# Second half of the tokens: second layer by seven block products over pairs of chunks, with stored first-layer weights

## The chip, the cores and the metric

The kernel runs on one NeuronCore of a Trainium2 chip. The metric is device time in microseconds (us) of one execution, the median of several runs. In the profile PE is TensorE (matmuls), PEld its weight loads, DVE VectorE, ACT ScalarE, POOL GpSimd and SP SyncE, which issues the DMAs here.

## What is computed

Clustered attention, then two feed-forward stages. The attention output (2 batches x 768 tokens, 8 heads x 64, so 1536 x 512) goes through a dense layer pair (512 to 2048, squared relu, 2048 to 512). The change touches the last stage alone, a mixture of 4 experts in which every token goes to every expert:

```python
def _moe2_ref(x, domain_probs, w1, w2):      # x 1536 x 512, w1 4 x 512 x 1024, w2 4 x 1024 x 512
    p = domain_probs / (domain_probs.sum(-1, keepdims=True) + 1e-09)
    out = np.zeros((N, D), dtype=np.float32)
    for e in range(E):
        h = np.maximum(x @ w1[e], 0.0)
        out += p[:, e:e + 1] * (h @ w2[e])
    return out
```

All is float32. A factor is split into a high half in the matmul's own format (fp32r) and a low half, the rest, and a product is made of three matmuls: high x high, high x low, low x high.

## The kernel before

In the last stage the tokens are done in two halves of 768, one after the other (NFQ = 16 chunks each, n = 0 to 15 and 16 to 31). A chunk is 256 of an expert's 1024 hidden columns; four chunks make an expert. For each chunk there is a group (`group`, L1652):

- **First layer**: the 512 x 256 weight block and the 768 tokens are cut into 2 x 2 blocks and multiplied by seven block products in place of eight (`PROD`, L890; `product`, L1023; `block_product`, L895). One is six matmuls of 384 columns. Chains A, B and C accumulate several products in one PSUM bank each, and ACT (`c_copy`, L1033) and DVE (`c_add`, L1036) take intermediate results out of them. Relu and the split into halves follow (`h_hi`, L1042, on ACT; `h_lo`, L1045, on DVE), into the tiles ga and gb.
- **Second layer**: six token tiles of 128 tokens (`token_tile`, L1080; `tile_products`, L1056), each six matmuls of 512 columns, and then an eviction on DVE (L1093) that multiplies by the token's probability and adds to the accumulator tile x2. The last one of all is split (`last_tile`, L1065).
- **Weights**: `fq_load` (L974) has SP load the chunk's two blocks into the tile raw. `fq_prep` (L992) makes the first layer's operands: plain blocks on ACT (L1005) and POOL (L1006), four sums on POOL (`w_sums`, L195), mixed blocks on ACT (L207) and POOL (L208). They lie in W["X"] and W["Y"], each with two halves by the parity of n. `second_hi` (L1014) and `second_lo` (L1017) split the second layer's block into W["Z"].

The second half of the tokens runs the same sixteen chunks again, weights included. Its first-layer token operands (`r_hi`, L967; `r_lo`, L970; tiles xa and rt) are made near the end of the first half; `swapped` (L1629) makes the last two in group 16, as products 4 and 3 of chunk 15 free their places.

The order of all instructions is written out by hand: each engine runs its own in the order in which the program issues them. In a group it is: products 4, (1), 3 of the chunks n - 1, n, n - 1; then 5, 6, 2, 7 of n; then the six token tiles of n - 1, with the preparation of chunk n + 1 between them. So products 3 and 4 of chunk n come one group later than its others:

```python
product(n, 1)                       # L1657
...
token_tile(n - 1, 0)                # L1681, behind product 7 of n
...
fq_load(n + 3, 0)                   # L1692
fq_load(n + 2, 1)
```

Of the kernel before, what the change touches and what calls it, by code (L numbers as in the profile page):

```python
# [34 lines left out]
def moe_attention_kernel(  # L35
# [178 lines left out]
    with tc.manual_schedule():  # L214
# [849 lines left out]

        def last_tile():  # L1065
            n, t = 2 * NFQ - 1, NTT - 1
            j = 2 * NTT - 1
            pc = pe_p[:, j, NFQ // NQ - 1:NFQ // NQ]
            acc, d = acc_j(1, t), ov[1, t].rearrange("p (a n) -> p a n", a=2)
            for m, (a, c0, c1) in enumerate(((0, 0, 256), (1, 0, 128), (1, 128, 256))):  # L1070
                o = bank[(7, 0, 2)[m]][:, 0:c1 - c0]
                tile_products(n, t, o, slice(a * 256 + c0, a * 256 + c1))
                x = acc[:, a, c0:c1]
                nc.vector.scalar_tensor_tensor(
                    out=x, in0=o, scalar=pc, in1=x, op0=ALU.mult, op1=ALU.add)
                if m != 1:
                    nc.sync.dma_start(
                        out=d[:, a] if m else d[:, 0], in_=acc[:, a])
# [618 lines left out]
        NN = 2 * NFQ  # L1697
        for n in range(NN):
# [44 lines left out]
```

## Time and profile before

| | us |
|---|---|
| median of 3 runs | 1007.53 |
| lowest and highest | 1006.74, 1007.82 |
| the profiled execution | 1007.97 |
| its span, first to last instruction | 1006.0 |
| granted TensorE clock | 0.999 of 2.4 GHz |

The span has roughly these stages: attention until about 250 us, the dense layer pair until about 505, the first half of the tokens in the last stage until about 744, and the second until the end. All times of the rows below count from the span's start. An entry of a list of groups has busy time, mean duration in ns, and the idle time ahead of it with what ended it; a duration holds the instruction's start and end phases, which overlap with its neighbours'.

### The profile page before, as it was taken

Reading aid. Unit: us, or ns where it says so; the run is one execution under the profiler, and the core shown is the slowest. Engines: PE = TensorE matmul, PEld = TensorE weight load, DVE = VectorE, ACT = ScalarE, POOL = GpSimd, SP = SyncE. Lnnn points to the kernel's source line nnn. Section 1 sums busy time; section 2 is a strip of 40 time slices with the busy share of each in tenths; the row PEclk is TensorE's granted clock in tenths of the full one; section 3 lists DMA queues with packets and bytes.
Section 4 is the critical chain, followed back from the end, with each engine's and each line's share of the span. In section 5 each row is a group of like instructions: output and inputs, shape, how many; then the busy total and the mean of one; then the engine's idle time right before and its main releaser. Section 6 shows DMA issues by size and latency. Waiting matters only on the chain.

```text
span 1006.0 us, 15008 instructions
## 1 busy us (share of the span) xinstructions
PE 998.3 (99%) x5469; PEld 893.7 (89%) x5469; DVE 734.4 (73%) x1126; ACT 560.2 (56%) x1131; POOL 607.8 (60%) x618
## 2 busy tenths in 40 slices
PE   8999999999999999999999999999999999999998
PEld 8999999999888888888889989899899898998997
DVE  6898999888899997898585555567676555555555
ACT  6888888888655654446554344344453443444431
POOL 6468777763326604347576766767678567676671
PEclk9999999999999999999999999999999999999999
DMA  7577876862112122212012212122123221221201
GB/s 186 128 157 178 205 172 165 178 140 72 42 43 84 45 82 84 85 42 83 22 43 85 61 65 84 42 85 65 62 84 119 71 84 43 84 67 60 84 22 63
DMA packets 74082, 89.65 MB, mean 89 GB/s; under 512 B 27332, under 2 KB 50264, under 8 KB 74008
## 3 DMA queue, kind: packets, MB, share of 16 engines
q1 hardware_dynamic: 74008, 88.69, 31.9%
q8 instruction: 43, 0.70, 0.3%
q14 instruction: 31, 0.25, 0.1%
HBM read 62.58 MB, written 3.19 MB: 65 GB/s over the span
## 4 chain that ended last, share of the span: by engine, by line
PE 95%; DVE 2%; POOL 1%; DMA 1%; ACT 1%; issue 0%; SPq 0%; POOLq 0%; ACTq 0%
PE bank L900 29%; PE bank L1062 26%; PE bank L931 13%; PE s L656 6%; PE t L689 6%; PE bank L878 5%; PE po L703 3%; PE po L705 3%; PE s L878 1%; PE m L478 1%; PE m L393 1%; PE po L1114 0%; DMA k<-nkh 0%; PE m L494 0%; DVE ptl L695 0%
## 5 line engine op out<-in xcount | busy, mean ns | idle before, releaser
L1093 DVE SCALAR_TENSOR_TENSOR x<-bank,pe_p,x 128x512 f32<-128x512 f32 x179 | 134.3, 751 | 67.4 <-PE bank L1062 67.2
L1006 POOL TENSOR_TENSOR wxl<-raw,wxh 128x512 fp32r<-128x512 f32 x64 | 82.5, 1310 | 139.7 <-ACT wxh L1005 139.7
L207 ACT CAST wyh<-raw 128x512 fp32r<-128x512 f32 x64 | 39.6, 621 | 152.0 <-POOL raw L200 120.4
L1062 PE MATMUL bank<-wzh,ga 128*128 128x512 f32 (+1 forms) x392 | 121.9, 386 | 0.0
L1062 PE MATMUL bank<-wzh,gb 128*128 128x512 f32 x384 | 121.2, 390 | 0.0
L1037 DVE TENSOR_TENSOR fa<-bank,fa 128x384 f32<-128x384 f32 x96 | 53.3, 556 | 85.5 <-PE bank L900 56.4
L695 DVE TENSOR_TENSOR ptl<-t,pth 128x384 fp32r<-128x384 f32 x192 | 98.1, 549 | 20.0 <-ACT pth L694 19.6
L900 PE MATMUL bank<-xa,wxh 128*128 128x384 f32 (+1 forms) x392 | 103.9, 346 | 0.0
L665 DVE TENSOR_REDUCE nb<-s 128x1 f32<-128x768 f32 x96 | 90.9, 948 | 8.4 <-PE s L656 8.0
L694 ACT CAST pth<-t 128x384 fp32r<-128x384 f32 x192 | 83.9, 486 | 9.3 <-PE t L689 8.4
L900 PE MATMUL bank<-xa,wyh 128*128 128x384 f32 (+1 forms) x344 | 88.6, 338 | 0.0
L676 ACT ACTIVATE p<-s,nb 128x768 f32<-128x768 f32 x96 | 88.0, 916 | 0.3 <-DVE nb L665 0.2
L656 PE MATMUL s<-k,q 80*128 80x384 f32 (+1 forms) x384 | 86.5, 346 | 0.2
L1062 PEld LDWEIGHTS bank<-wzh,ga 128*128 128x128 f32 x392 | 73.3, 188 | 14.5
L689 PE MATMUL t<-identf,p 128*128 128x128 f32 x576 | 85.4, 276 | 0.4 <-DVE ptl L695 0.3
L1062 PEld LDWEIGHTS bank<-wzh,gb 128*128 128x128 f32 x384 | 72.1, 188 | 14.7
L208 POOL TENSOR_TENSOR wyl<-raw,wyh 128x512 fp32r<-128x512 f32 x64 | 84.6, 1342 | 0.0
L1034 ACT COPY fa<-bank 128x384 f32<-128x384 f32 x96 | 46.1, 480 | 66.1 <-PE bank L900 66.0
L703 PE MATMUL po<-pth,vv 128*128 128x256 f32 x288 | 80.4, 309 | 0.0
L931 PE MATMUL bank<-gb,wzh 128*128 128x512 f32 x240 | 78.0, 391 | 0.2
L900 PEld LDWEIGHTS bank<-xa,wxh 128*128 128x128 f32 x392 | 72.2, 188 | 5.6
L689 PEld LDWEIGHTS t<-identf,p 128*128 128x128 f32 x576 | 67.6, 140 | 9.5 <-DVE ptl L695 6.8
(290 smaller groups left out, 2640.8 us busy)
## 6 DMA issues: line engine op xcount, KB each, us to landing
raw<-in_moe_w_dram SPq DMA_DIRECT2D x64, 512.0 KB, 3.6
raw<-in_moe_w_in_dram SPq DMA_DIRECT2D x7, 1024.0 KB, 5.2
raw<-in_moe_w_out_dram SPq DMA_DIRECT2D x6, 1024.0 KB
k<-nkh SPq DMA_DIRECT2D x28, 192.0 KB, 3.3
q<-nqh SPq DMA_DIRECT2D x28, 192.0 KB, 4.1
nv<-in_v_dram SPq DMA_DIRECT2D x16, 192.0 KB, 4.1
out_dram<-x SPq DMA_DIRECT2D x11, 256.0 KB, 2.0
k<-nkl SPq DMA_DIRECT2D x14, 192.0 KB, 3.4
```

Source lines behind the costliest of these rows:

```text
L208: return lambda: eng.tensor_tensor(lo, a[m], hi.bitcast(F32), op=ALU.subtract)
L656: nc.tensor.matmul(s[:, j, 0:HALF], stk[i, nq][:, t * 128:(t + 1) * 128], stk[i, nk][:, j * HALF:(j + 1) * HALF], start=first, stop=not first)
L665: nc.vector.tensor_reduce(out=nb, in_=s_ps[u][:, :, 0:HALF], axis=AX.XY, op=ALU.max, negate=True)
L676: nc.scalar.activation(p, s_ps.pop(u)[:, :, 0:HALF], AF.Exp, bias=nb_t.pop(u), accum_out=sums_t[hp][:, i % 2, t:t + 1])
L689: nc.tensor.transpose(tp[:, j], p_sb[u][:, half, j * 128:(j + 1) * 128], identf)
L694: return (lambda: nc.scalar.copy(dh, tp), lambda: nc.vector.tensor_tensor(dl, tp, dh.bitcast(F32), op=ALU.subtract))
L695: lambda: nc.vector.tensor_tensor(dl, tp, dh.bitcast(F32), op=ALU.subtract))
L703: nc.tensor.matmul(po_t[pr], vt[i][:, kt], pth[:, kt], start=(kt == 0), stop=False)
L900: nc.tensor.matmul(ps, w[:, ks], x(xx)[:, kt], start=(first and kt == 0 and z == 0), stop=(kt == 1 and z == 2), skip_group_check=True)
L931: nc.tensor.matmul(o, a[:, d], b, start=(ft == 0 and z == 0), stop=(ft == 1 and z == 2))
L1062: nc.tensor.matmul(o, a, w[:, f, cols], start=(f == 0 and z == 0), stop=(f == 1 and z == 2))
L1093: nc.vector.scalar_tensor_tensor(out=acc, in0=o, scalar=pc, in1=acc, op0=ALU.mult, op1=ALU.add)
```

## The change

In the second half of the tokens:

- The second layer is done for two chunks (a pair m, 512 hidden columns) at once: tokens 2 x 384, hidden columns 2 x 256, output columns 2 x 256, by the same seven block products in the order 1, 5, 6, 2, 7, 3, 4 (`second_product`). A product is three row tiles, each six matmuls of 256 columns and an eviction of 256 columns. The evictions add each chain's intermediate state to the output block that it belongs to. Each chain and row tile has a PSUM bank (B shares bank 4 for two).
- Its operands are sums and differences of blocks: on the token side S5, S3 on DVE, S6, S7 on POOL, high halves H on ACT, low halves L on DVE; on the weight side sums t on POOL, high halves y on ACT, low halves z on POOL. Tables say behind which product (0 to 6) of which stretch each is issued (`SECOND`, `NEXT`, `LATE`, `LAST`, `START2`).
- The order is: chunk 16's seven products, the six token tiles of chunk 15, chunks 17, 18, 19; then the second layer of pair m and the first layer of the two chunks of pair m + 2, in turn; at the end the second layers of pairs 6 and 7. Chunk 16's products 3 and 4 come right behind its product 7.
- First-layer weights are not prepared again: for chunks 2 to 15 the finished operands of the first half are stored in DRAM (`keep`, six DMAs for 14 blocks of 128 KB) and loaded again (`back`). Chunks 16 and 17 are prepared as before. The second layer's weights are loaded a pair at a time (`load_second`, 1 MB).

```diff
@@ fq_load, fq_prep @@
-            if n >= 2 * NFQ:
+            if n >= NFQ + (2 if part == 0 else 0):
                 return
...
-            if n >= 2 * NFQ:
+            if n >= NFQ + 2:
                 return [lambda: None] * 3
@@ last_tile removed, a DRAM pool added @@
-        def last_tile():
...
+        mp["hb"] = mctx.enter_context(tc.tile_pool(name="hb", bufs=1, space=bass.MemoryType.DRAM))
@@ end of group(n), and what follows it @@
+            keep(n + 1)
             fq_load(n + 3, 0)
             fq_load(n + 2, 1)
...
+        ORDER2 = (1, 5, 6, 2, 7, 3, 4)
+        kept = {n: mp["hb"].tile([128, 4096], F32, name=f"kept{n}") for n in range(2, NFQ)}
+        KEPT = [("X", 0, 2), ("Y", 0, 4), ("X", 3, 4)]
+
+        def keep(n):
+
+            if n not in kept:
+                return
+            p = (n % 2) * 1024
+            for t, a, b in KEPT:
+                for x in range(2):
+                    o = 2048 * (t == "Y") + x * 1024
+                    nc.sync.dma_start(
+                        out=kept[n][:, o + a * 256:o + b * 256],
+                        in_=W[t][x][:, p + a * 256:p + b * 256].bitcast(F32))
+
+        def back(n, parts=KEPT):
+
+            if n >= 2 * NFQ:
+                return
+            p = (n % 2) * 1024
+            for t, a, b in parts:
+                for x in range(2):
+                    o = 2048 * (t == "Y") + x * 1024
+                    nc.sync.dma_start(
+                        out=W[t][x][:, p + a * 256:p + b * 256].bitcast(F32),
+                        in_=kept[n - NFQ][:, o + a * 256:o + b * 256])
...
+        def load_second(m):
+
+            if m >= NFQ // 2:
+                return
+            e, q = divmod(m, NQ // 2)
+            nc.sync.dma_start(
+                out=raw_t["q", 0].rearrange("p (k f) -> p k f", k=4),
+                in_=moe2_w2[e, q * 2 * FQ:(q + 1) * 2 * FQ, :].rearrange("(k p) f -> p k f", p=128))
...
+        def y_sum(m, i):
+            x, y = {5: ("12", 1), 6: (3, 5), 7: (3, "12"), 4: (2, 6)}[i]
+            nc.gpsimd.tensor_tensor(y_val(m, i), y_val(m, x), y_val(m, y), op=ALU.subtract)
+
+        def y_hi(m, i):
+            nc.scalar.copy(y_op(i, 0), y_val(m, i))
+
+        def y_lo(m, i):
+            nc.gpsimd.tensor_tensor(
+                y_op(i, 1), y_val(m, i), y_op(i, 0).bitcast(F32), op=ALU.subtract)
...
+        def h_sum(m, i, eng=nc.vector):
+            if i == 5:
+                nc.vector.scalar_tensor_tensor(
+                    out=hsum(m), in0=hx(m, 1, 1), scalar=0.0, in1=hx(m, 1, 0), op0=ALU.max, op1=ALU.add)
+            elif i == 3:
+                nc.vector.scalar_tensor_tensor(
+                    out=hx(m, 0, 1), in0=hx(m, 0, 1), scalar=0.0, in1=hx(m, 0, 0),
+                    op0=ALU.max, op1=ALU.subtract)
+            elif i == 7:
+                eng.tensor_tensor(hx(m, 1, 0), hx(m, 0, 0), hx(m, 1, 0), op=ALU.subtract)
+            else:
+                eng.tensor_tensor(hx(m, 0, 0), hsum(m), hx(m, 0, 0), op=ALU.subtract)
+
+        def h_hi2(m, i):
+            if i in (2, 4):
+                nc.scalar.activation(h_op(i, 0), h_val(m, i), AF.Relu)
+            else:
+                nc.scalar.copy(h_op(i, 0), h_val(m, i))
+
+        def h_lo2(m, i, eng=nc.vector):
+            hi = h_op(i, 0).bitcast(F32)
+            if i in (2, 4):
+                nc.vector.scalar_tensor_tensor(
+                    out=h_op(i, 1), in0=h_val(m, i), scalar=0.0, in1=hi, op0=ALU.max, op1=ALU.subtract)
+            else:
+                eng.tensor_tensor(h_op(i, 1), h_val(m, i), hi, op=ALU.subtract)

+        def first_product(n, hooks={}):
+
+            m, q = divmod(n - NFQ, 2)
+            for x, i in enumerate(ORDER2):
+                product(n, i)
+                a, b, c = [pb[n, z][:, 0:HALF] for z in "ABC"]
+                if i == 1:
+                    nc.scalar.copy(hx(m, 0, q)[:, 0], a)
+                elif i == 5:
+                    nc.scalar.copy(hx(m, 1, q)[:, 1], c)
+                elif i == 6:
+                    nc.scalar.copy(hx(m, 1, q)[:, 0], a)
+                elif i == 4:
+                    nc.scalar.activation(hx(m, 0, q)[:, 1], a, AF.Relu)
+                else:
+                    o, z = {2: (hx(m, 0, q)[:, 0], b), 7: (hx(m, 1, q)[:, 1], a), 3: (hx(m, 1, q)[:, 0], c)}[i]
+                    nc.vector.tensor_tensor(o, z, o, op=ALU.add)
+                if n == NFQ + 1:
+                    back(n + 2, [W_AT[i]])
+                if n == NFQ and i == 1:
+                    third(n - 1)
+                    last_relu(n - 1)
+                if q == 0 and x == 4:
+                    h_relu(m, 0)
+                if q == 1 and x == 1:
+                    h_relu(m, 1)
+                for f in hooks.get(x, []):
+                    f()
+            if n != NFQ + 1:
+                back(n + 2)
...
+        def second_product(m, hooks={}):
+
+            e = m // (NQ // 2)
+            last = m == NFQ // 2 - 1
+            for x, i in enumerate(ORDER2):
+                r, d = BLOCK[i]
+                b = PROD[i][2]
+                for j in range(3):
+                    o = {"A": bank[5 + j][:, 0:256], "C": bank[(1, 3, 2)[j]][:, 0:256],
+                         "B": bank[(4, 0, 4)[j]][:, 256 * (j == 2):][:, 0:256]}[b]
+                    js = slice(j * 128, (j + 1) * 128)
+                    for f in range(2):
+                        hh, hl = [h_op(i, z)[:, f, js] for z in range(2)]
+                        wh, wl = [y_op(i, z)[:, f] for z in range(2)]
+                        for z, (a, w) in enumerate(((hh, wh), (hh, wl), (hl, wh))):
+                            nc.tensor.matmul(
+                                o, a, w, start=(i in (1, 5, 2) and f == 0 and z == 0),
+                                stop=(f == 1 and z == 2), skip_group_check=True)
+                    t = 3 * r + j
+                    pc = pe_p[:, NTT + t, e:e + 1]
+                    acc = acc_half(t, d)
+                    if m == 0 and i in (1, 5, 6, 4):
+                        nc.vector.tensor_scalar(acc, o, pc, None, op0=ALU.mult)
+                    else:
+                        nc.vector.scalar_tensor_tensor(
+                            out=acc, in0=o, scalar=pc, in1=acc, op0=ALU.mult, op1=ALU.add)
+                    if last and i in (2, 7, 3, 4):
+                        nc.sync.dma_start(out=ov[1, t][:, 256 * d:256 * d + 256], in_=acc)
+                for f in hooks.get(x, []):
+                    f()
+
+        def call(f, *a):
+            return lambda: f(*a)
+
+        def table(m, rows):
+            fs = {"H": h_hi2, "L": h_lo2, "S": h_sum, "y": y_hi, "z": y_lo, "t": y_sum}
+
+            def one(w):
+                if w[0] == "R":
+                    return call(load_second, m + 1)
+                f = call(fs[w[0]], m, int(w[1]))
+                return call(fs[w[0]], m, int(w[1]), nc.gpsimd) if w[2:] else f
+            return {x: [one(w) for w in ws.split()] for x, ws in rows.items()}
+
+        SECOND = {0: "H1 y1 S5 L1 z1 t5 S7g S6g", 1: "H5 L5", 2: "y5 z5 t6", 3: "H2",
+                  4: "H6 y6 y2 z6 z2 t4 t7", 5: "H7", 6: "H4 y3 z3"}
+        NEXT = [{0: "L2 S3 L6", 2: "y7 y4 H3 z7 z4", 6: "L7 R"}, {0: "L3 L4"}]
+        LATE = {0: "H1 y1 S5 L1 z1 t5 S7g S6g", 1: "H5 L5", 2: "y5 z5 t6", 3: "H2 L2",
+                4: "H6 y6 y2 z6 z2 t4 t7 S3 L6", 5: "H7", 6: "H4 y3 z3 H3"}
+        LAST = {0: "L7", 1: "y7 y4 z7 z4 L3", 2: "L4"}
+        START2 = [{0: "y5 z5 t6", 2: "y6 y2 z6 z2 t4 t7", 6: "y3 z3"},
+                  {0: "H1 S5 L1 S7g S6g", 1: "H5 L5", 2: "H2 y7 y4 z7 z4", 6: "H6 H7 L2 S3 R"},
+                  {0: "H4 L6 L7", 2: "H3", 6: "L3 L4"}]
...
+        first_group()
+        for n in range(1, NFQ):
+            group(n)
+        load_second(0)
+        fourth(NFQ - 1)
+        prep = fq_prep(NFQ + 1)
+        first_product(NFQ, {1: prep[0:2]})
+        then = table(0, {3: "y1 z1 t5"})
+        then[1] = prep[2:]
+        for t in range(NTT):
+            token_tile(NFQ - 1, t)
+            for f in then.get(t, []):
+                f()
+        for n in range(3):
+            first_product(NFQ + 1 + n, table(0, START2[n]))
+        NM = NFQ // 2
+        for m in range(NM):
+            if m + 1 < NM:
+                rows = SECOND if m + 2 < NM else LATE
+                second_product(m, table(m + 1, rows))
             else:
-                first_group()
-        fourth(NN - 1)
-        third(NN - 1)
-        last_relu(NN - 1)
-        for t in range(NTT - 1):
-            token_tile(NN - 1, t)
-        last_tile()
+                second_product(m, table(m, LAST))
+            for q in range(2):
+                n = NFQ + 2 * m + 4 + q
+                if n < 2 * NFQ:
+                    first_product(n, table(m + 1, NEXT[q]))
```

## Rows read from the trace of the kernel before

**Rows 1.** The page: busy time and share of an engine; data moved in 40 slices.
```profile
PE 998.3 (99%) x5469; PEld 893.7 (89%) x5469; DVE 734.4 (73%) x1126; ACT 560.2 (56%) x1131; POOL 607.8 (60%) x618
...
GB/s 186 128 157 178 205 172 165 178 140 72 42 43 84 45 82 84 85 42 83 22 43 85 61 65 84 42 85 65 62 84 119 71 84 43 84 67 60 84 22 63
```
**Rows 2.** Chain of waits, in order of time: start, length, engine, tile and line.
```profile
518.57 8.20 PE bank L1062 x36
526.77 7.30 PE bank L900 x42
...
994.07 8.86 PE bank L1062 x48
```
**Rows 3.** List of PE's waits, whole span: us in total, times, longest.
```profile
PE po L1114 <- DVE sel L299: 2.6, 1, 2.6
```
**Rows 4.** Timeline of PE: start, length; nine starts in attention, four in the last tile.
```profile
254.07 0.28 PE L705 MATMUL po<-ptl,vv 128*128 128x256 f32 x1
...
255.02 0.28 PE L705 MATMUL po<-ptl,vv 128*128 128x256 f32 x1
...
1001.87 0.27 PE L1062 MATMUL bank<-wzl,ga 128*128 128x128 f32 x1
...
1002.20 0.28 PE L1062 MATMUL bank<-wzl,ga 128*128 128x128 f32 x1
```
**Rows 5.** Groups by shape, 510 to 1006 us; the POOL one from 250 to 512.
```profile
L1093 DVE SCALAR_TENSOR_TENSOR x<-bank,pe_p,x 128x512 f32<-128x512 f32 x179 | 134.3, 751 | 67.4 <-PE bank L1062 67.2
L1037 DVE TENSOR_TENSOR fa<-bank,fa 128x384 f32<-128x384 f32 x94 | 52.2, 557 | 85.3 <-PE bank L900 56.4 <-ACT fa L1034 28.8
L971 DVE TENSOR_TENSOR rt<-x,rt 128x768 fp32r<-128x768 f32 x3 | 2.8, 945 | 0.0
...
L1074 DVE SCALAR_TENSOR_TENSOR x<-bank,pe_p,x 128x256 f32<-128x256 f32 x1 | 0.5, 483 | 0.0
...
L207 ACT CAST wyh<-raw 128x512 fp32r<-128x512 f32 x62 | 38.5, 621 | 152.0 <-POOL raw L200 120.4 <-POOL raw L202 31.6
...
L968 ACT CAST xa<-x 128x768 fp32r<-128x768 f32 x3 | 2.5, 825 | 0.0
...
L971 POOL TENSOR_TENSOR xa<-x,xa 128x768 fp32r<-128x768 f32 x2 | 3.7, 1847 | 0.0
```
**Rows 6.** Timeline of POOL and of DVE about the start of the second half.
```profile
742.93 0.74 POOL L201 TENSOR_TENSOR raw<-raw 128x256 f32<-128x256 f32 x1
...
744.45 2.55 POOL L208 TENSOR_TENSOR wyl<-raw,wyh 128x512 fp32r<-128x512 f32 x2
746.96 2.40 POOL L1019 TENSOR_TENSOR wzl<-raw,wzh 128x1024 fp32r<-128x1024 f32 x1
749.31 2.17 POOL L971 TENSOR_TENSOR xa<-x,xa 128x768 fp32r<-128x768 f32 x1
...
737.76 0.55 DVE L1046 SCALAR_TENSOR_TENSOR ga<-fa,ga 128x384 fp32r<-128x384 f32 x1
...
748.20 1.58 DVE L1046 SCALAR_TENSOR_TENSOR ga<-fa,ga 128x384 fp32r<-128x384 f32 x1 [0.59 <-ACT ga L1043]
749.70 2.61 DVE L971 TENSOR_TENSOR xa<-x,xa 128x768 fp32r<-128x768 f32 x1
```
**Rows 7.** Timeline of ACT and of PE there; L1062 begins a token tile.
```profile
749.18 0.48 ACT L1034 COPY fa<-bank 128x384 f32<-128x384 f32 x1 [0.29 <-PE bank L900]
...
751.01 0.39 PE L1062 MATMUL bank<-wzh,ga 128*128 128x512 f32 x1
```
**Rows 8.** DMA issues (size, us to landing); timeline of ACT and POOL, one group.
```profile
raw<-in_moe_w_dram SPq DMA_DIRECT2D x64, 512.0 KB, 3.6
...
690.71 0.91 ACT L1005 CAST wxh<-raw 128x512 fp32r<-128x512 f32 x2
...
697.17 3.26 POOL L208 TENSOR_TENSOR wyl<-raw,wyh 128x512 fp32r<-128x512 f32 x2
```

More of the change, by code (lines that the diff above doesn't have):

```diff
@@ L1063, in tile_products @@
                         o, a, w[:, f, cols], start=(f == 0 and z == 0), stop=(f == 1 and z == 2))
-        def last_tile():
[L1066 to L1078, printed above, removed]
         def token_tile(n, t):
@@ L1695, in group @@
                 t_sum(1, (RT3, RT1, RT2, None, RT4)[m])
-        NN = 2 * NFQ
-        for n in range(NN):
+        ORDER2 = (1, 5, 6, 2, 7, 3, 4)
[11 more added lines that the diff above has]
+                        in_=W[t][x][:, p + a * 256:p + b * 256].bitcast(F32))
@@ new lines, in back @@
+        def back(n, parts=KEPT):
[8 more added lines that the diff above has]
+                        in_=kept[n - NFQ][:, o + a * 256:o + b * 256])
+        W_AT = {1: ("X", 0, 1), 5: ("Y", 3, 4), 6: ("Y", 0, 1), 2: ("X", 1, 2),
+                7: ("Y", 2, 3), 3: ("Y", 1, 2), 4: ("X", 3, 4)}
@@ new lines, in moe_attention_kernel, with hx, hsum @@
+        fa8 = fa.rearrange("p (k t) -> p k t", k=8)
+        ga, gb = gs
+        def hx(m, r, q):
+            if m % 2:
+                return x2_t[r][:, q, 0:S].rearrange("p (f t) -> p f t", f=2)
+            return fa8[:, ((0, 3), (2, 5))[r][q]:][:, 0:((2, 2), (5, 3))[r][q]:((1, 1), (4, 2))[r][q]]
+        def hsum(m):
+            o = (m % 2) * NR
+            return raw_t["q", 1][:, o:o + NR].rearrange("p (f t) -> p f t", f=2)
+        H_AT = {1: (xa, 2 * NR), 5: (xa, 4 * NR), 6: (xa, 6 * NR), 2: (xa, 8 * NR),
+                7: (ga, 0), 3: (ga, 2 * NR), 4: (gb, 0)}
@@ new lines, in moe_attention_kernel, with h_op, y_op @@
+        (z0h, z0l), (z1h, z1l) = W["Z"]
+        Y_AT = {1: ((z0h, 0), (z0l, 0)), 5: ((z0h, 512), (z0l, 512)),
+                6: ((gb, 1536), (gb, 2048)), 2: ((gb, 2560), (gb, 3072)),
+                7: ((ga, 3072), (ga, 3584)), 3: ((z1h, 0), (z1l, 0)), 4: ((z1h, 512), (z1l, 512))}
+        def h_op(i, x):
+            t, o = H_AT[i]
+            return t[:, o + x * NR:o + (x + 1) * NR].rearrange("p (f t) -> p f t", f=2)
+        def y_op(i, x):
+            t, o = Y_AT[i][x]
+            return t[:, o:o + 512].rearrange("p (f d) -> p f d", f=2)
@@ new lines, in load_second, with y_val, blk @@
+        def load_second(m):
[5 more added lines that the diff above has]
+                in_=moe2_w2[e, q * 2 * FQ:(q + 1) * 2 * FQ, :].rearrange("(k p) f -> p k f", p=128))
+        def y_val(m, i):
+            def blk(q, d):
+                return raw_t["q", 0].rearrange("p (k f) -> p k f", k=4)[
+                    :, 2 * q:2 * q + 2, 256 * d:256 * d + 256]
+            if i == 6:
+                return raw_t["q", 1][:, 2 * NR:].rearrange("p (f d) -> p f d", f=2)
+            return {1: blk(0, 0), 5: blk(0, 0), 7: blk(0, 1), 2: blk(1, 0), 4: blk(1, 0), 3: blk(1, 1),
+                    "12": blk(0, 1)}[i]
@@ new lines, in y_sum, with h_val @@
+        def y_sum(m, i):
[6 more added lines that the diff above has]
+                y_op(i, 1), y_val(m, i), y_op(i, 0).bitcast(F32), op=ALU.subtract)
+        def h_val(m, i):
+            return {1: hx(m, 0, 0), 5: hsum(m), 6: hx(m, 0, 0), 2: hx(m, 0, 1), 7: hx(m, 1, 0),
+                    3: hx(m, 0, 1), 4: hx(m, 1, 1)}[i]
@@ new lines, in h_relu @@
+        def h_relu(m, r):
+            x = hx(m, r, 0)
+            if r == 0:
+                x = x[:, 0]
+            nc.scalar.activation(x, x, AF.Relu)
+        def h_sum(m, i, eng=nc.vector):
[10 more added lines that the diff above has]
+                eng.tensor_tensor(hx(m, 0, 0), hsum(m), hx(m, 0, 0), op=ALU.subtract)
@@ new lines, in acc_half @@
+        def acc_half(t, d):
+            if t < 4:
+                return x2_t[t // 2][:, t % 2, S + 256 * d:S + 256 * d + 256]
+            return x2_t[t - 4][:, d, S + 512:2 * S]
+        BLOCK = {1: (0, 0), 5: (1, 1), 6: (0, 1), 2: (0, 0), 7: (1, 1), 3: (0, 1), 4: (1, 0)}
+        def second_product(m, hooks={}):
[27 more added lines that the diff above has]
+                    f()
@@ L1699, in moe_attention_kernel @@
+        for n in range(2 * NFQ):
             pb[n, "A"] = bank[n % 2]
```

2 lines of the change are left out of this document (removed).

## The prediction

> **What bounds the kernel now.** I read the page first: the matrix engine, PE, is busy 99% of the span, the next one 73% [rows 1]. A busy PE need not be a paced one, so I read the chain of waits next. In the second half of the token work it is PE and nothing else: 42 first-layer matmuls take 7.30 us, 36 second-layer matmuls 8.20 us, group after group [rows 2], and in the list of PE's waits four entries stand, all of attention's lines, the longest 2.6 us [rows 3]. So the time there is the number of matmuls times their pace, and an edit gains only what it takes out of that, less any new wait of PE. The pace is start-to-start time, not the duration in the list: 8.20/36 = 0.228 us for 512 columns, 7.30/42 = 0.174 us for 384. For 256 columns, eight steps in attention take 0.95 us, so 0.119 us, and I use 0.120. For 128 columns three steps of the last tile take 0.33 us, 0.11 us each [rows 4]: below 256 columns nearly nothing is won by making a matmul shorter.
>
> **The matmuls.** The change leaves the first layer's count as it is and replaces two chunks' 72 matmuls of 512 columns by 7 products x 3 row tiles x 6 = 126 of 256 columns. Before: 16 x 8.20 = 131.2 us. After: 8 x 126 x 0.120 = 121.0 us. Gain 10.2 us. Columns alone would say 12.5% of 131.2, or 16.4 us; more and shorter matmuls give 6 us of that back. The split last tile (8.86 us where a whole group takes 8.20, rows 2) goes too: 0.7 us. Together **-10.9 us**. The operand shapes are those of the attention rows (128x128 held, 256 columns moving), so I allow 0.118 to 0.122 us, 2 us either way.
>
> The Trainium skill (TensorE: Matmul & The Clock Gate, "Back-to-back issue gap") gives an isolated gap of columns/2.4 plus 2.5 ns; as an estimate from it, 576 x 0.2158 less 1008 x 0.1092 would be a gain of 14.2 us. The rows differ from it here, 0.228 and 0.120 us, and the sum goes by them.
>
> **What must now be ready in time.** The second layer's operands are no longer plain copies. Per pair of chunks, by the diff: VectorE (DVE) has 21 evictions of 256 columns, 6 additions of 384, and 9 operations of 768 columns with both inputs in SBUF (seven low halves L, sums S5 and S3). POOL has 11 operations of 512 columns (seven z, four t) and 2 of 768 (S7, S6). ACT has 7 casts of 768, 7 of 512 and 10 copies or relus. Durations [rows 5 to 7]: DVE 0.48 us per eviction, 0.56 per addition, 0.95 per 768, each less 0.08 where it follows another (749.70 lies 0.08 before 748.20 + 1.58); POOL 0.74, 1.27 (2.55 for two), 1.85 and 2.40 us for 256, 512, 768 and 1024 columns; ACT 0.48 for a copy, 0.62 and 0.83 for the casts, less 0.1 in a row. A pair lasts 2 x 7.30 + 15.1 = 29.7 us. DVE needs 21 x 0.41 + 6 x 0.48 + 9 x 0.87 = 19.3, POOL 11 x 1.27 + 2 x 1.85 = 17.7, ACT about 14 us. Each fits by itself.
>
> DVE and POOL are not independent, though. A DVE operation of 384 columns with two SBUF inputs took 0.55 us at 737.76; at 748.20 it took 1.58 and ended 0.42 us after POOL's subtraction of 746.96; at 749.70 a 768-column one took 2.61 us and ended 0.83 us after POOL's operation of 749.31. That one in turn took 2.17 us for 1.85, as DVE ended at 749.78 [rows 5, 6]. They take turns, each for a whole instruction. Evictions from PSUM have a mean of 0.751 us over 179, so they take no part. So the 9 x 0.8 and 17.7 us add up: 25 of 29.7 us. Still a fit over a pair, but a DVE operation waits up to 1.2 us for its turn, with the evictions and additions queued behind it, and for these PE waits, since an accumulating chain can't go on in a bank that has not been read.
>
> **Waits that I expect.**
> *First chunk of the second half (16).* Product 3 moves from the next group to right behind product 7. Its moving operand's low half (xa, 768 columns) was ready at 749.70 + 2.61 = 752.31 [rows 6]; product 7 ended at 751.01, where a token tile began [rows 7]. Also ACT's two casts for chunk 17 now stand ahead of the copy of 749.18 that product 7 needs; that wait overlaps. I take **+1.3 us**, between 0 and 2.6 (DVE's turn coming first, or one POOL operation later).
> *Fill.* Three first-layer chunks follow one another (17, 18, 19) while the first pair's operands are made. On ACT the casts H6 and H7 stand ahead of the first copy of chunk 19, and H6 waits for POOL's S6. POOL from 752.3: chunk 17's weights 2.0 + 3.2 + 2.55, nine operations x 1.27, S7 and S6 3.7: 22.9 us; three DVE turns (S5, L1, L5) 2.4; idle until ACT's casts y5 and y6, which stand behind copies of chunk 17, about 2.5 by the same queue count. S6 ends at 780.1, H6, H7 and the copy at 781.9. PE: products 3 and 4 until 754.4, six token tiles 8.2, chunks 17 and 18 14.6, two products of 19 2.1: 779.3, and product 6 then wants that copy. **+2.6 us**, between 0 (POOL 2.6 us earlier) and 5 (S6 two POOL operations and a turn later).
> *Drain.* The last two second-layer blocks follow one another, so pair 7's operands are made under pair 6's matmuls alone. DVE there: 21 x 0.41 = 8.6 us, six two-input operations 5.2, and for these about 0.8 us of turn each, as POOL never rests: 4.9. That is 18.7 us against 15.1 plus about 1.1 of lag that is harmless. **+2.5 us**, between 0 and 5.
> *The six pairs between* I cost at nothing: 14.6 us of first-layer products follow each second-layer block, and POOL's and DVE's arrears are worked off there. If that cover is too thin, this is the second rival.
> *End.* The last eviction has 256 columns for 128; by 0.75 and 0.48 us for 512 and 256 [rows 5] that is +0.1. The output piece behind it is 128 KB in both.
>
> **Stored weights.** Chunks 2 to 15 store 14 blocks of 128 KB, 1.8 MB each, in a group of 15.5 us: 118 GB/s on top of 42 to 85 in most slices; a slice early in the kernel moved 205 [rows 1]. The last store waits for POOL's low halves, over at 697.17 + 3.26 = 700.43; the same half of the tile is cast again one group after 690.71, at 706.2 [rows 8]. 5.8 us stand against the 3.6 us that 512 KB took to land [rows 8], so nothing is lost; if they didn't suffice, ACT waits 3.9 us per group for POOL ahead of its next cast (120.4 us for 62 casts, two per group, rows 5). Six more issues on SP stand ahead of the next loads, which have a whole group to land; POOL's queue carries no DMA. In the second half the loads return 2 x 1.8 + 1 MB per 29.7 us, 159 GB/s, each chunk over 15 us ahead of its use. Chunk 19 comes block by block behind chunk 17's products. Cost 0. The weight preparation that goes away was off the path and returns nothing by itself; it is what makes room on POOL.
>
> **Sum.** -10.9 + 1.3 + 2.6 + 2.5 + 0.1 = -4.4 us. The profiled execution took 1007.97 us, 2.0 around a span of 1006.0 and 0.44 above the median of 1007.53, so nothing in the difference hangs on which is taken: 1003.1 us.
>
> **Rivals.**
> *All covered.* The fill's and drain's waits are small enough that I may have put them one POOL operation too late each; then only the matmuls show: 996.6, and up to 998.5 with part of the first wait. For it: no wait of PE in this stretch today. Against: the turns [rows 6].
> *The turns bind in every pair: slower.* Place: the start of each even chunk, where L2, S3 and L6 on DVE each wait for POOL's t and z operations, with the bank-clearing additions behind them, and ACT's copies stand behind casts that wait for POOL (y6 behind t6). Price: about one turn, 1.2 us, for each of six pairs, 7.2 us: 1010.3 us. It decides from 0.7 us per pair, where the gain is gone, and passes 0.2% from 1.1 us. For: 25 of 29.7 us is a tight fit for one resource. Against: nothing must be ready for more than a block ahead. The Trainium skill (SBUF — State Buffer, "Who interferes with whom") calls this an exclusive lock held for the whole instruction. The trace agrees, with 1.58 and 2.61 us for operations of 0.55 and 0.95.
> *Stores or returned loads stand in the way.* If a store lands 1 us after the cast needs the tile beyond ACT's idle time, in 13 groups of the first half: -4.4 + 13 = 1016 us. Against: 5.8 us and 4 us of cover.
> *The change doesn't bring the pace.* If 256 columns ran at 0.131 us, the second layer would cost what it did. Rows 4 speak against it; this is inside what is left over.
>
> **Numbers.** Forecast case (waits at fill and drain) 0.42, all covered 0.22, turns in every pair 0.24, stores 0.07, the rest 0.05. About 0.2%, 2 us, is what a measurement of this kernel tells from no change: below 1005.5 lie all of the covered case, 0.38 of the forecast and 0.02 of the rest: 0.62 faster. Between are 0.04, 0.12 and 0.01: 0.17 the same. Slower: 0.12, 0.07 and 0.02: 0.21. The range goes from the covered case, 996.5, to just beyond the price of turns in every pair, 1011; the likeliest case alone is 1000 to 1006.
>
> **What would show it.** Right: second-layer blocks of 126 matmuls in 15.1 us in the chain; PE's new waits named DVE or ACT and grouped at chunk 16, chunk 19 and between the last two blocks, 6.4 us together; no wait on a DMA. Wrong: PE waits of over 0.7 us at each even chunk, a pace off 0.120 us, a group of the first half longer than 15.5 us, or no waits at all.

## The result, and the profile after

The changed kernel takes **1019.14 us** (median of 4 runs, 1017.59 to 1019.6) against 1007.24 us for the kernel before (4 runs, 1006.74 to 1007.82): ratio 1.0115, 95% interval 1.0098 to 1.0133. The forecast was 1003.1 us, with a range from 996.5 to 1011. The kernel is slower, and it lies beyond the range. The profiled execution took 1017.59 us for a span of 1015.6.

The page of the changed kernel, to be held beside [rows 1]:

```profile
PE 994.0 (98%) x5889; PEld 906.9 (89%) x5889; DVE 798.2 (79%) x1204; ACT 576.0 (57%) x1139; POOL 632.9 (62%) x594
...
GB/s 184 129 159 177 198 187 164 175 154 39 46 38 83 84 43 83 84 83 42 21 135 161 212 179 174 207 166 198 187 155 124 158 187 187 119 100 156 187 42 63
...
PE 77%; POOL 13%; DVE 5%; ACT 2%; issue 2%; POOLq 0%; ACTq 0%; DVEq 0%
```

PE does 4.3 us less work, yet the span is 9.6 us longer: PE now waits. The chain that ended last has POOL in it for 13% of the span; a slice of GB/s is 25.4 us, so the stores take the first half of the token work (from about 505 us) up to 212 GB/s, and the loads take the second (from about 743 us) up to 187. The four largest entries in the list of PE's waits from 740 us on (us in total, times, longest), where there was none before [rows 3], name who is late:

```profile
PE bank L1863 <- DVE x L1872: 4.1, 9, 2.3
PE bank L900 <- DVE x L1826: 3.2, 4, 1.0
PE bank L900 <- ACT x L1817: 3.1, 1, 3.1
PE bank L900 <- DVE fa L1826: 3.0, 3, 1.0
```

L1863 is the second layer's matmul, L1872 its eviction; L900 is the first layer's matmul, L1826 the addition and L1817 the copy that read its banks. No wait names a DMA.

I cut the second half into its stages at the starts of PE's rows: each block of 126 second-layer matmuls, and the 84 first-layer matmuls of two chunks between two blocks. The forecast's pace [rows 2, rows 4] is the ideal. The six token tiles of chunk 15, behind chunk 16's stretch, take 8.20 us as before.

| stage | us | ideal | lost | forecast |
|---|---|---|---|---|
| chunk 16's stretch, 54 matmuls | 10.75 | 9.39 | 1.36 | 1.3 |
| fill, three chunks | 27.34 | 21.9 | 5.4 | 2.6 |
| six pairs, 15.54 + 15.97 each | 189.0 | 178.2 | 10.8 | 0 |
| drain, two blocks | 34.19 | 30.24 | 3.95 | 2.5 |

Lost are 21.5 us for 6.4 forecast (0.1 at the end aside); 10.9 us were to be won. That leaves +10.6, and the second half is in fact 10.4 us longer than before (742.87 to 1015.6 against 743.70 to 1006.0). Half of the loss stands in the row that the forecast priced at nothing. One pair by windows (length, then busy us and instructions of PE, PEld, DVE, ACT, POOL; granted clock, DMA share, GB/s), the second-layer block and the first-layer part:

```profile
820.65:836.19 15.54, 15.37 (x128) 15.17 (x127) 11.56 (x23) 6.47 (x10) 10.93 (x7) 1.00 0.60 225
836.19:852.16 15.97, 14.99 (x87) 14.53 (x85) 13.92 (x13) 7.86 (x15) 10.79 (x7) 1.00 0.23 80
```

No engine beside PE is full in either, and the clock is at 2.4 GHz throughout. So it is not capacity. The timelines show two things that are late.

First, the head of the even chunk. DVE has L2, S3 and L6 there, three operations of 768 columns with two SBUF inputs, and then three additions that empty PE's banks; POOL runs z and t weights at the same time:

```profile
836.79 1.99 DVE L1805 SCALAR_TENSOR_TENSOR xa<-fa,xa 128x768 fp32r<-128x768 f32 x1
838.89 1.86 DVE L1788 SCALAR_TENSOR_TENSOR fa<-fa 128x768 f32<-128x768 f32 x1
840.67 2.04 DVE L1808 TENSOR_TENSOR xa<-fa,xa 128x768 fp32r<-128x768 f32 x1
842.64 1.48 DVE L1826 TENSOR_TENSOR x<-bank,x 128x384 f32<-128x384 f32 x3
```

and POOL's timeline beside it:

```profile
835.40 2.56 POOL L1770 TENSOR_TENSOR gb<-raw,gb 128x512 fp32r<-128x512 f32 x2 [0.73 <-ACT gb L1767]
838.04 3.86 POOL L1764 TENSOR_TENSOR raw<-raw 128x512 f32<-128x512 f32 x2
841.86 1.99 POOL L1770 TENSOR_TENSOR wzl<-raw,wzh 128x512 fp32r<-128x512 f32 x1
```

Without a turn to wait for, such a DVE operation takes 0.95 us (826.32 in the same timeline) and such a POOL operation 1.3 (2.56 for two). Here each DVE operation lasts its own time and most of one of POOL's: 5.85 us from 836.79 to the first addition, for 2.7 us of work. PE waits 1.0 us for the second of these additions:

```profile
843.70 0.62 PE L900 MATMUL bank<-xa,wxh 128*128 128x384 f32 x2 [0.98 <-DVE x L1826]
```

The page's groups (count, busy, mean ns) answer to [rows 5]: the evictions, which read PSUM, keep their 0.48 us, and POOL's low halves take 1.83 for 1.3.

```profile
L1770 POOL TENSOR_TENSOR wzl<-raw,wzh 128x512 fp32r<-128x512 f32 x32 | 58.6, 1831 | 64.8 <-ACT wzh L1767 64.8
...
L1872 DVE SCALAR_TENSOR_TENSOR x<-bank,pe_p,x 128x256 f32<-128x256 f32 x156 | 71.0, 480 | 30.0 <-PE bank L1863 30.0
```

Second, inside the second-layer block, where the timeline of PE shows a wait at the third row tile of product 2:

```profile
828.89 0.98 PE L1863 MATMUL bank<-gb,xa 128*128 128x256 f32 x6 [0.17 <-DVE x L1872]
```

Product 2 has its three row tiles in bank 4, bank 0 and the other half of bank 4. The third waits until the first has been evicted, and that eviction stands on DVE behind L5 (826.32, 0.95). In e8, below, the block without this is 15.11 us for 15.54: a wait listed with 0.17 us costs 0.43, as the six matmuls start 0.33 us late and take 0.82 us for 0.72.

### The profile page after: what moved, and what is told of

The parts are those of the page before. It is cut to its first block, busy times and chain, and to the rows that moved or that the text cites. A ratio compares the mean times of both kernels' runs of the same rounds, so it can differ in the third digit from the quotient of the medians.

```text
span 1015.6 us, 16401 instructions
## 1 busy us (share of the span) xinstructions
PE 994.0 (98%) x5889; PEld 906.9 (89%) x5889; DVE 798.2 (79%) x1204; ACT 576.0 (57%) x1139; POOL 632.9 (62%) x594
## 4 chain that ended last, share of the span: by engine, by line
PE 77%; POOL 13%; DVE 5%; ACT 2%; issue 2%; POOLq 0%; ACTq 0%; DVEq 0%
PE bank L900 22%; PE bank L931 12%; PE bank L1062 11%; PE s L656 6%; PE t L689 6%; PE bank L878 5%; POOL raw L1764 5%; PE po L703 3%; PE po L705 3%; PE bank L1863 3%; POOL gb L1770 2%; DVE x L1872 1%; POOL wzl L1770 1%; PE s L878 1%; PE m L478 1%
## 5 line engine op out<-in xcount | busy, mean ns | idle before, releaser
L900 PE MATMUL bank<-xa,wxh 128*128 128x384 f32 (+1 forms) x392 | 104.6, 348 | 6.2 <-DVE x L1826 3.2
L1770 POOL TENSOR_TENSOR wzl<-raw,wzh 128x512 fp32r<-128x512 f32 x32 | 58.6, 1831 | 64.8 <-ACT wzh L1767 64.8
L1078 DVE SCALAR_TENSOR_TENSOR x<-bank,pe_p,x 128x512 f32<-128x512 f32 x90 | 67.6, 751 | 36.4 <-PE bank L1062 36.4
L1872 DVE SCALAR_TENSOR_TENSOR x<-bank,pe_p,x 128x256 f32<-128x256 f32 x156 | 71.0, 480 | 30.0 <-PE bank L1863 30.0
L1006 POOL TENSOR_TENSOR wxl<-raw,wxh 128x512 fp32r<-128x512 f32 (+1 forms) x36 | 47.1, 1328 | 70.1 <-ACT wxh L1005 70.1
L900 PE MATMUL bank<-xa,wyh 128*128 128x384 f32 (+1 forms) x344 | 88.9, 338 | 0.3 <-DVE xa L971 0.3
L900 PEld LDWEIGHTS bank<-xa,wxh 128*128 128x128 f32 x392 | 70.9, 188 | 12.9 <-DVE x L1826 4.5
L900 PE MATMUL bank<-rt,wyh 128*128 128x384 f32 (+1 forms) x264 | 72.5, 356 | 3.5 <-ACT x L1817 3.1
L705 PE MATMUL po<-ptl,vv 128*128 128x256 f32 x288 | 72.5, 281 | 0.0
L900 PE MATMUL bank<-xa,wxl 128*128 128x384 f32 (+1 forms) x196 | 67.8, 346 | 0.0
L207 ACT CAST wyh<-raw 128x512 fp32r<-128x512 f32 x36 | 22.3, 622 | 78.7 <-POOL raw L200 61.3
L900 PEld LDWEIGHTS bank<-xa,wyh 128*128 128x128 f32 x344 | 62.4, 188 | 1.9 <-DVE xa L971 0.7
L656 PEld LDWEIGHTS s<-k,q 80*128 80x128 f32 (+1 forms) x384 | 63.3, 189 | 0.6 <-ACT p L676 0.2
```

The costliest lines, as they stand in the source:

```text
L656: nc.tensor.matmul(s[:, j, 0:HALF], stk[i, nq][:, t * 128:(t + 1) * 128], stk[i, nk][:, j * HALF:(j + 1) * HALF], start=first, stop=not first)
L705: nc.tensor.matmul(po_t[pr], vt[i][:, kt], ptl[:, kt], start=False, stop=(kt == NTT - 1))
L900: nc.tensor.matmul(ps, w[:, ks], x(xx)[:, kt], start=(first and kt == 0 and z == 0), stop=(kt == 1 and z == 2), skip_group_check=True)
L1770: nc.gpsimd.tensor_tensor(y_op(i, 1), y_val(m, i), y_op(i, 0).bitcast(F32), op=ALU.subtract)
```

## Experiments

**e1: do the stores and loads cost anything?** The kernel before, with the first layer's weights stored and read back as the change does it, and the old second half.

```diff
+            keep(n + 1)
             fq_load(n + 3, 0)
             fq_load(n + 2, 1)
```

> The second half as before, with plain second-layer products, but its first-layer weights stored in the first half and loaded again. Theory (turns): the matrix engine's work is that of before and DVE and POOL have less to do, so 1007 us, within 2 of before, and groups of 15.50 us in both halves. Rival (stores and loads stand in the way): over 1009.5 us, with first-half groups longer than 15.50 us or matmuls waiting for a DMA.

1007.28 against 1007.68 us, ratio 0.9998 (0.9988 to 1.0007). PE has no wait in the token work, and a group keeps its 15.50 us in both halves. The transfers cost nothing, and the preparation that goes away returns nothing by itself.

**e2: is it POOL's weights?** From the second pair on, the low halves z and the differences t are left out, so the second layer multiplies by stale weights there.

```diff
+                if m and w[0] in "zt":
+                    return lambda: None
```

> The changed kernel; from pair 1 on POOL's weight operations (z and t, 11 of its 13 per pair) are left out, so those pairs use pair 0's low halves and unsummed blocks. ACT and DVE have the same instructions. Theory (turns at the port that DVE and POOL share): the 768-column operations on DVE fall to about 0.95 us, a pair of 31.5 us falls to 29.7 to 30.0, the drain of 34.2 to 30.3 to 31.5; the fill, pair 0's, stays at 27.3. Span about 1015.6 - 10.5 - 3 = 1002. Rival (POOL's chain is late and ACT's casts wait for it): the same fall. Rival (DVE has simply too much work between the evictions): a pair stays at 31.3 to 31.5 us and the span over 1014.

1008.95 us in a single execution. A pair's two windows (columns as before):

```profile
818.47:834.49 16.02, 15.36 (x128) 15.15 (x127) 12.04 (x23) 6.54 (x10) 4.87 (x2) 1.00 0.30 111
834.49:849.12 14.63, 14.63 (x86) 14.63 (x85) 9.13 (x13) 7.46 (x14) 0.00 (x0) 1.00 0.59 214
```

The first-layer part is without a wait, 14.62 us in the mean for 15.97: 1.35 us a pair. The block, however, went from 15.54 to 16.02: S7 and S6 now run earlier on POOL, onto L5, which took 1.44 us for 0.95, and PE waits 0.7 us for the eviction behind it, at the shared half of bank 4. So a pair is 30.65 us, and the 29.7 to 30.0 expected were missed.

**e3: is it POOL's time or its reading?** From the second pair on, POOL's operations for t and z become three writes of constants each, about as long and at the same place; the second layer computes with these.

```diff
+        def blank(t, k):
+            for c in range(3):
+                nc.gpsimd.memset(t[:, :, 0:(256, 256, 128)[c]], 0.001 * k)
         def y_sum(m, i):
+            if m:
+                return blank(y_val(m, i), i)
...
         def y_lo(m, i):
+            if m:
+                return blank(y_op(i, 1).bitcast(F32), 0)
```

> The changed kernel; from pair 1 on each z and t on POOL is replaced by three fills of the same place (256, 256 and 128 columns twice), which read nothing and should take POOL about 1.2 us together, as the operation did alone; the second layer then works with constants there. So POOL is as busy as before but reads nothing. Theory (turns): a pair falls to 29.7 to 30.2 us and the 768-column DVE operations take about 0.95 us except beside S7 and S6. Rival (POOL's chain is late): POOL's chain is as long as it was, so a pair stays above 30.8 us with matmuls or ACT waiting for POOL.

1017.28 us in a single execution: little gain in sum, with a pair at 31.33 us, where the rival had put it. The windows show that the reason is another one:

```profile
822.39:839.11 16.72, 15.36 (x127) 15.15 (x127) 12.74 (x23) 6.74 (x10) 13.59 (x24) 1.00 0.29 107
839.11:853.72 14.61, 14.61 (x86) 14.61 (x85) 9.13 (x13) 7.46 (x14) 5.07 (x12) 1.00 0.58 213
```

The first-layer part is 14.61 us, although POOL is at work there, and the three DVE operations take the 0.95 us that they take without a turn. POOL's and DVE's timelines there:

```profile
837.48 2.90 POOL L1764 MEMSET raw<- 128x512 f32 x6
840.32 1.48 POOL L1764 MEMSET wzl<- 128x512 f32 x3
841.74 1.48 POOL L1764 MEMSET ga<- 128x512 f32 x3
...
839.72 0.95 DVE L1813 SCALAR_TENSOR_TENSOR xa<-fa,xa 128x768 fp32r<-128x768 f32 x1
840.78 0.96 DVE L1796 SCALAR_TENSOR_TENSOR fa<-fa 128x768 f32<-128x768 f32 x1
841.65 0.95 DVE L1816 TENSOR_TENSOR xa<-fa,xa 128x768 fp32r<-128x768 f32 x1
```

So it is POOL's reading that makes them take turns. The block grew to 16.7: S7, which still reads, falls on L5 (2.14 us), and PE waits 1.4 us at bank 4. The kernel has two limits, and moving POOL trades one for the other. The fill, which is the changed kernel's own here, took 28.49 us for 27.34; the last section returns to that.

**e4: the fill.** The casts H6 and H7 and the operations behind them go behind chunk 19's first copies.

```diff
-2: "H2 y7 y4 z7 z4", 6: "H6 H7 L2 S3 R"}, {0: "H4 L6 L7", 2: "H3", 6: "L3 L4"}]
+2: "H2 y7 y4 z7 z4", 6: "L2 R"}, {0: "H4", 2: "H6 H7 S3 H3", 6: "L6 L7 L3 L4"}]
```

> The changed kernel; in the fill, casts H6 and H7 are issued behind chunk 19's third copy and not ahead of its first one, and S3, L6, L7 behind them. Theory: the 3.1 us wait of the matrix engine for that copy goes, and with it the stretch of twelve matmuls at half clock behind it (1.8 us); some of it comes back as a wait for L6 in pair 0's second-layer block or for the copies. The fill falls from 27.3 to 22.5 to 24.5 us, the time by 3 to 5 us, to about 1015. Rival (the whole of POOL's arrears has to be waited for somewhere): the fill and pair 0's block together shorten by less than 1 us.

1015.48 us, ratio 1.0081 (1.0066 to 1.0096). The fill fell from 27.34 to 22.66 us, the first block paid 1.3 back and the drain 1.2. In the changed kernel that wait had been followed by a stretch at a lower clock (columns as before, the clock is the third number from the end):

```profile
782.20:785.00 2.80, 2.74 (x12) 2.74 (x13) 2.80 (x3) 2.80 (x6) 1.23 (x1) 0.73 0.18 21
785.00:787.00 2.00, 2.00 (x8) 2.00 (x7) 0.68 (x2) 0.17 (x1) 0.00 (x0) 0.52 0.92 325
787.00:789.00 2.00, 2.00 (x14) 2.00 (x13) 1.17 (x3) 0.00 (x0) 0.00 (x0) 1.00 0.99 328
```

**e5, e6, e7: less for POOL.** The weights of products 1, 2 and 3 are plain blocks, so their halves can be stored in the first half and read back (token B); POOL loses three z of its eleven weight operations. e6 adds e4's fill, e7 also moves t6 and S3.

```diff
-        SECOND = {0: "H1 y1 S5 L1 z1 t5 S7g S6g", 1: "H5 L5", 2: "y5 z5 t6", 3: "H2",
-                  4: "H6 y6 y2 z6 z2 t4 t7", 5: "H7", 6: "H4 y3 z3"}
+        SECOND = {0: "H1 B1 S5 L1 t5 S7g S6g", 1: "H5 L5", 2: "y5 z5 t6", 3: "H2",
+                  4: "H6 y6 B2 z6 t4 t7", 5: "H7", 6: "H4 B3"}
```

> The changed kernel; the second layer's three weight operands that are plain blocks (1, 2 and 3) are stored as finished halves in the first half of the tokens and loaded, so per pair POOL has z1, z2 and z3 and ACT y1, y2 and y3 less. Nothing else moves. Theory (turns): the port's load per pair falls by 3 x 1.27 = 3.8 us, from 25.4 to 21.6 of 29.7; a pair falls from 31.5 to 29.8 to 30.6 us, the fill from 27.3 to 23 to 24.5 (three POOL operations less ahead of S6, and no half-clock stretch), the drain from 34.2 to 31.5 to 33. Time 1003 to 1007 us. Rival (only the clash of one DVE operation with S7 and S6 counts, and it moves with them, as in the run without z and t): a pair stays at 30.6 or above and the time at 1008 or above. Rival (the extra stores, 0.75 MB a group, get in the way): first-half groups longer than 15.50 us.

> The kernel of the run before, with the other order in the fill (H6, H7 behind chunk 19's third copy). Theory: what the wait for that copy still costs goes, 0 to 2 us less than the run before; 1002 to 1006 us.

> The kernel of the run before, with t6 ahead of S7 and S6 on POOL, so that these come later than L5 on DVE, and in the drain S3 and L6 one product later each. Theory (turns): L5 takes 0.95 us, the drain loses 1 to 2 us, a pair stays or falls by up to 0.5; 1000 to 1005 us. Rival (the order doesn't matter, only the load does): within 0.5 us of the run before.

1012.95 us (1.0055), 1013.88 (1.0062) and 1015.21 (1.0078): all three missed their ranges. In all three the first-layer part of a pair is 14.6 us and the block 16.0: as in e2, the turns are gone from the one and bank 4 is left in the other. In e7, L5 is at 1.44 us all the same. All three gave some 5 us back in the first half (in e5 the second half begins at 748.04 for 742.87): the store of chunk 0's halves was issued too late, and ACT's next cast waited for it, as e5's list of waits shows:

```profile
ACT wzh L1015 <- DMA keptz<-wzh: 5.6, 1, 5.6
```

So their times say less of the second half than their windows do.
Against e5, e6 and e7 won 0.8 us in the fill (22.9 and 23.0 us for 23.7) and lost more in the first block (20.01 and 18.70 us for 16.02).

**e8: one bank index.** Product 2's third row tile goes from bank 4 to bank 1. Product 3's sum, which goes on from product 5's, lies open in that bank's other half, and for that row tile product 5's share is lost from it (see the last section).

```diff
-                         "B": bank[(4, 0, 4)[j]][:, 256 * (j == 2):][:, 0:256]}[b]
+                         "B": bank[(4, 0, 1)[j]][:, 256 * (j == 2):][:, 0:256]}[b]
```

> The changed kernel with one index changed: the third row tile of product 2 accumulates in the free half of bank 1 and no longer in the half of bank 4 beside the first row tile, whose eviction it waited for. Theory (turns and a shared bank): the direct waits at that place (0.17 us in a pair, more where DVE is late) go, and DVE gets on with the rest earlier; a pair falls from 31.5 to 30.4 to 31.1 us, the drain by 0.5 to 1, the time by 4 to 7 us, to 1012 to 1015. Rival (turns alone): the direct waits are only 1.5 us in all, so the time falls by 0 to 2 us.

1011.59 us, ratio 1.0037 (1.0024 to 1.0051): 7.5 us from one index, a little more than expected. Its trace shows 6.6 us less in the six pairs and 0.7 more in the drain; what the medians differ by beyond these 5.9 us is not accounted for. The windows of a pair:

```profile
820.23:835.34 15.11, 15.11 (x127) 15.11 (x127) 11.57 (x23) 6.05 (x10) 10.50 (x7) 1.00 0.74 278
835.34:850.64 15.30, 15.05 (x86) 14.49 (x85) 13.67 (x13) 8.04 (x16) 11.93 (x7) 1.00 0.14 39
```

The block is 0.43 us shorter. The first-layer part is shorter too, by 0.67 us, though POOL does the same there: against PE, POOL's z operations now start 0.44 us later, L2 comes before the second of them instead of behind it, and takes 1.16 us for 1.97 (at 805.54; the same operation of the changed kernel at 805.30). Who gets the first turn is worth 0.8 us.

**e9, e10, e11: both limits at once.** e9 is e5 with e8's bank and an earlier store; e10 is e9 with another drain table; e11 is e3 with e8's bank. e8's words on product 3 hold for all three, e3's on the constants for e11.

> Stored halves of the second layer's plain operands, with the bank apart as in the run before, and the first store of the second layer's halves issued a group earlier on SP (it held up chunk 2's cast, and with it the matrix engine for 5.5 us in the first half). Theory: a pair at 29.7 to 30.0 us (port's load 21.6 of 29.7, no shared bank), the fill at 23.7, the drain at 31.5 to 33; first-half groups 15.50. Time 1000 to 1003.5 us, faster than the kernel before. Rival (DVE's own work is too much for the second-layer block): a pair stays above 30.4 us and the time above 1005.

> The kernel of the run before, in the drain t6 ahead of S7 and S6, and S3 and L6 one product later each. Theory: the drain falls to 30.3 to 31.5 us; 999 to 1002 us. Rival (order doesn't matter): as the run before.

> The bank apart and, from pair 1 on, POOL's weight operations replaced by fills of the same places, which read nothing (the second layer works with constants there). Theory (turns and a shared bank are the whole of it): a pair at 29.7 to 30.0 us, no wait of the matrix engine in pairs 1 to 6. Rival (something else is left, such as DVE's own work): a pair over 30.4 us.

1001.52 us (0.9939, 0.9925 to 0.9953), 1000.38 (0.9927, 0.9914 to 0.9941) and 1001.77 in a single execution. A pair is 29.74, 29.7 and 29.7 us, and no wait of PE is left in the pairs. The drain of e10 is 31.40 us for e9's 31.92.

**e13: the bank alone, with the whole computation.** Products in the order 1, 5, 6, 3, 7, 2, 4; product 2's third row tile takes bank 1 after product 3's chain there has been evicted. Product 2's operand and weights are then made two products later, in the drain's tables as well.

```diff
-            for x, i in enumerate(ORDER2):
+            for x, i in enumerate((1, 5, 6, 3, 7, 2, 4)):
...
-                         "B": bank[(4, 0, 4)[j]][:, 256 * (j == 2):][:, 0:256]}[b]
+                         "B": bank[(4, 0, 1)[j]][:, 0:256]}[b]
...
-2: "y5 z5 t6", 3: "H2",
-                  4: "H6 y6 y2 z6 z2 t4 t7", 5: "H7", 6: "H4 y3 z3"}
+2: "y5 z5 t6",
+                  4: "H6 y6 z6 t7", 5: "H7 H2 y2 z2 t4", 6: "H4 y3 z3"}
...
```

> The changed kernel with the order 1, 5, 6, 3, 7, 2, 4 and bank 1 for product 2's third row tile, and nothing else: POOL still builds all seven weights of the second layer. Nothing of the computation is left out. If the shared bank is worth about 1.1 us a pair by itself, as between the changed kernel and e8, a pair is 30.2 to 30.7 us and the time 1010 to 1014. If that price came from the disturbed chain, the pair stays at 31.3 to 31.7 and the time at 1017 to 1020.

1018.32 us, ratio 1.0119 (1.0103 to 1.0134): no gain. These are the numbers of the second expectation, but not its reason: the block is 15.10 us, as in e8, so the bank's price there did not come from product 3's disturbed sum. But the first-layer part is 16.39 for 15.97: the casts H2 and y2 now stand in ACT's burst at the head of the chunk, ahead of the copy that empties PE's first bank. PE's timeline:

```profile
837.91 0.62 PE L900 MATMUL bank<-rt,wyh 128*128 128x384 f32 x2 [0.98 <-ACT x L1817]
...
842.60 0.62 PE L900 MATMUL bank<-xa,wxh 128*128 128x384 f32 x2 [0.25 <-DVE x L1826]
```

**e12: both repairs, with the whole computation.** e10's stored weights and a drain table after its pattern, e13's order and bank.

> The changed kernel with the second layer's weights z and t read back as in e9, and the seven products in the order 1, 5, 6, 3, 7, 2, 4, so that product 2's third row tile has bank 1, after product 3's chain there has been evicted, instead of the other half of bank 4. Nothing of the computation is left out. If the shared bank and the shared port are what the pairs lost, a pair is 29.6 to 29.9 us as in e9, the fill 23 to 24.5, the drain 30.5 to 33, and the time 999 to 1003 us, ratio 0.993 to 0.997. If e9's gain on the bank came from the disturbed chain of product 3, the pair stays at 30.4 to 30.7 and the time is 1007 to 1009.

**1000.08 us** (999.19 to 1000.2) against 1007.22: ratio **0.9926, 0.9913 to 0.9938**. It beats both kernels. The fill is 23.71 us, a pair 15.10 + 14.60, the drain 30.76. Its chain in the pairs is PE alone, as it was before the change [rows 2]:

```profile
831.15 14.59 PE bank L900 x84
845.75 15.11 PE bank L1887 x126
860.85 14.60 PE bank L900 x84
```

and PE's waits from 740 us on come to 1.9 us:

```profile
PE bank L900 <- DVE x L1850: 0.7, 1, 0.7
PE bank L900 <- ACT fa L1845: 0.4, 1, 0.4
PE bank L900 <- ACT x L1841: 0.3, 1, 0.3
PE bank L900 <- DVE xa L971: 0.3, 1, 0.3
PE bank L1887 <- issue: 0.2, 1, 0.2
```

## Why the prediction was wrong

**The matmuls: right.** A block without waits is 15.10 us (126 x 0.120), the 10.2 us of the forecast. e12's pairs and chain show the forecast gain in full.

**Stores and loads, and the preparation that goes: right.** e1 measured nothing for either, and no wait of PE names a DMA.

**Chunk 16: right**, 1.36 for 1.3 us. PE's two waits there, 0.4 us for ACT's copy and 0.3 for DVE's xa, stand where the forecast had them.

**Fill: mis-sized.** The wait was named rightly (PE on ACT's copy behind H6 and H7) and nearly sized: that copy ended at 782.22 for 781.9, a gap of 3.25 us for 2.6. Unforeseen was what followed: 12 matmuls took 3.65 us for 2.09, most of them at half clock with 0.32 us each for 0.174: 1.6 us more. A wait for an addition took 0.4, and restarts the last 0.2.

**Drain: mis-sized**, 3.95 for 2.5. DVE's run of L2, S3, L6 and evictions did make PE wait, 2.3 us once (2.5 with the restart), which is the forecast's term; the two waits for bank 4 come on top, 0.4 and 0.8 us with the restart. That these two are a price of their own is not shown: e8 has neither, but its one wait is 2.8 us and its drain 34.9.

**The step that failed: "the six pairs between I cost at nothing".** They cost 1.8 us each, 10.8 us in all, and this turns the sign. The working compared totals, 25 of 29.7 us at the shared port, and concluded that arrears would be worked off. But the port's work comes in a burst. L2, S3 and L6 are issued back to back at the head of the even chunk, each behind a POOL operation, and the additions that PE needs stand behind all three. What counted was the 5.85 us of this burst against the moment when the bank is wanted, not the sum over the pair.

Two mechanisms share the 1.8 us. The turns take 1.35: e2 and e3 bring the first-layer part to 14.6 us, and e3 shows that POOL's reading, not its being busy, is what counts. This was the second rival, at the place that it named and with DVE and POOL as it named them, priced at 1.2 us a pair; it was given 0.24. (Its other part, ACT's copies behind casts that wait for POOL, does not show: in the pairs PE waits for DVE alone.) The rest, 0.43, is bank 4, shared by two row tiles of product 2, which no part of the prediction mentions; the diff showed it. For the pairs the prediction asked when banks are read on the first layer's side alone. The two are not independent: with the bank alone repaired e8 gains 1.09 us a pair, as the order of turns changes with it, and with the turns alone repaired the block's wait grows to 0.9 (e2, e5) or 1.6 us (e3). Only both together give 29.7.

The rival's own forecast, 1010.3 us, lacks the bank (6 x 0.43), the dearer turn (6 x 0.15), and what the fill (2.8) and the drain (1.45) cost beyond their terms: 7.7 us, which leads to 1018.0.

The Trainium skill (SBUF — State Buffer, "Who interferes with whom") says that a VectorE instruction with two SBUF inputs contends with a GpSimd instruction that reads SBUF, and not with one that only writes it. The trace agrees on both sides: 1.86 to 2.04 us beside POOL's subtractions, 0.95 beside its memsets.

Open: that the place of H2 and y2 in ACT's queue is what e13 lost is read from its trace; H2 was not moved back by itself, as its operand's place is only free after product 2.

## What to carry to other kernels

Two engines that take turns must be costed burst by burst: list what the consumer waits for at each point, and put a full turn of the other engine before each operation queued ahead of it; a sum over the period only says that the work can fit. When a change splits a PSUM bank between two chains, count the eviction of the first as something the second waits for. And when two waits hang on the same engine's queue, repair both before judging either, as the repair of one can lengthen the other: here a pair of 31.5 us became shorter by 0.2 to 0.9 us with fewer turns alone (e3, e2, e5), by 1.1 or nothing with the bank alone (e8, e13), and by 1.8 with both.

## What was not expected of the hardware

After the fill's wait of 3.08 us PE's granted clock was 0.73 and then 0.52 over the next stretches, and most of 12 matmuls ran at 1.2 GHz. The same wait, 3.06 to 3.08 us at the same place, left the clock at 1.00 in e2, e11 and e13 (fills of 25.9 us). In e8 it fell again (27.3), and in e3 for longer (28.5). Two windows some 2 us behind that wait, of e13 and of e3:

```profile
784.60:786.60 2.00, 2.00 (x13) 1.81 (x12) 1.66 (x3) 0.91 (x2) 0.00 (x0) 1.00 0.72 189
784.90:786.90 2.00, 2.00 (x8) 2.00 (x8) 0.81 (x1) 1.21 (x2) 0.00 (x0) 0.50 0.78 201
```

One and the same wait cost up to 2.6 us more in some kernels than in others, each seen in one execution; what decides was not tried.

In e8 a chain started in one half of a bank while the other half held an open sum, and that sum was lost: e8's output differs from the reference by 0.3235 (relative), and the reference without product 5's share of that row tile differs from the whole one by the same 0.3235. The Trainium skill (PSUM — Partial Sum Buffer, "The four PSUM rules") says that two accumulation groups open at once in the same bank and quadrant of partitions cannot both begin with the clearing flag. e8's output agrees; no time hangs on it.
